# Denominators of linear attention: eight token tiles taken ahead into the accumulation of G

## The chip, the cores and the metric

The kernel runs on one core of a Trainium2 chip. A core has a matrix engine (TensorE, PE in the profile, with weight loads as PEld), three engines for vectors (VectorE or DVE, ScalarE or ACT, GpSimd or POOL), and a queue that issues transfers (SyncE, SP). Each engine works through its own list of instructions in order, and waits on semaphores where an operand comes from another engine. The metric is the time of one execution on the device in microseconds. Before the change it is 810.38 us, the median of three runs (808.94 to 812.14).

## The reference

Two kinds of layers alternate over x, of 2048 tokens by 640 features in fp32: Fourier mixing and linear attention, each twice, each behind a layer norm and with a residual.

```python
def _A_ref(x, dft_seq_re, dft_seq_im, dft_hid_re, dft_hid_im):
    a = einsum("bsd,ed->bse", x, dft_hid_re)
    b = einsum("bsd,ed->bse", x, dft_hid_im)
    return einsum("ts,bse->bte", dft_seq_re, a) - einsum("ts,bse->bte", dft_seq_im, b)

def _B_ref(x, wqkv, wo):                       # 32 heads of 20 features
    q, k, v = heads of x @ wqkv
    phi = lambda t: where(t > 0, t + 1, exp(t)) + 1e-6
    pq, pk = phi(q), phi(k)
    kv = einsum("bhsd,bhse->bhde", pk, v)
    z = einsum("bhsd->bhd", pk)                # sum of the keys over all tokens
    num = einsum("bhqd,bhde->bhqe", pq, kv)
    den = einsum("bhqd,bhd->bhq", pq, z)[..., None] + 1e-6
    return (num / den, heads joined) @ wo

x = x + A(layernorm(x)); x = x + B(layernorm(x))
x = x + A(layernorm(x)); x = x + B(layernorm(x))
```

The change concerns `den`: for each token and head, the product of the token's 20 query features with z, summed, plus 1e-6.

## The kernel before, in words

The tokens lie in 16 tiles of 128 partitions by 640 features, and stay in SBUF throughout. Matrix products that need fp32 are made of three products of a high and a low part (`split`: ACT copies the high part, DVE subtracts it to get the low one). The Fourier layers fold the tokens into symmetric parts first; folding for the second Fourier layer runs beside the outputs of the first attention layer, mostly on POOL and DVE, with statistics on ACT.

One attention layer (`Attention.keys_values`) works in these stages:

- Keys and queries for a group of tiles. The first group has ten tiles (0 to 9), the second six (10 to 15). A tile is normed, transposed, multiplied by the key weights and by the query weights, and both go through phi. Query tiles are kept (`self.PQ`); the query of the last tile is left for later (`late`). POOL adds each key tile to a running sum, `pksum` (line 295).
- G for the same group (`gram`, line 251): 30 matmuls a tile take the normed tile transposed with its keys into four PSUM buffers. DVE norms the tile once more (line 127), ACT and DVE make high and low parts of the tile (xh, xl) and of its keys (ph, pl; lines 133 and 134); this is `gram_ready`, called one tile ahead. xn, xh, xl and ph take four of the 12 buffers of the temporary pool (`temp`, tag "tmp").
- With tile 10, the first of the second group, `total` adds ten small matmuls (line 350) that sum `pksum` over the partitions into unused columns of the same PSUM buffers. After the second group `total_out` copies these sums with ACT into a tile zb (lines 359 and 360): z, the same in every partition.
- Combining (`combine`): G is combined with the value weights (line 390) and masked by heads, and then multiplied by the output weights, of which ACT and DVE make the parts. The result is the matrix M of a layer. In between stand the late query and the first weighted queries.
- Outputs (`outputs`): tile by tile, the weighted query is transposed, split, multiplied by M, and DVE adds the result to x (line 490).

A weighted query takes two functions. `weigh` (line 434) multiplies the query by zb on POOL. `weighted` reduces the product over the 20 features of a head to 32 denominators per token (line 447, DVE), adds 1e-6 (line 448, DVE), takes reciprocals (line 449) and multiplies the query by them in two pieces (lines 451 and 457). `weigh` is called three tiles ahead of the output it is for, `weighted` two tiles ahead.

The order in which the instructions of an engine stand is not the order of the source: the tile framework schedules them by a simulated timeline and priorities, which `k.ahead(...)` shifts for single steps (the table `AHEAD`). Only SP's order is by hand, and in the Fourier parts the vector engines'. Buffers of a pool are handed out in turn, and a new tile in a buffer waits for the last use of the old one.

In layer 0, DVE also compares symmetric halves of the Fourier matrices piece by piece (`Check`, lines 1033 and 1050), in steps placed among the tiles; `verdict` evaluates this in the last stage.

Of the kernel before, what the change touches and what calls it, by code (L numbers as in the profile page):

```python
# [8 lines left out]
F32 = mybir.dt.float32  # L9
F32R = mybir.dt.float32r  # L10
AF = mybir.ActivationFunctionType
ALU = mybir.AluOpType
AX = mybir.AxisListType

S, D, H, DH = 2048, 640, 32, 20
# [29 lines left out]
VLOWS = (0, 0, 1, 0)  # L45
WLOWS = ((5, 2), (1, 1))
GATE = 2
AHEAD = {'0out00': -60, '2keep00': -60, '2out10': -600, '1q13': 60, '2keep01': 600, '2keep02': 5, '0kv0': 5, '2out02': -20, '0out10': -600, '0keep00': -5, '1q14': 60, '0w1': 5, '2out01': 20, '0kv2': -600, '0m1': -5, '0kv5': 60, '1weigh15': -20, '0out12': -200, '1res13': 5, '2m1': -20, '0keep10': 60, '0weigh0': 60, '0first': -5, '2out12': -200, '2weigh1': 5, '2first': 60, '0m3': 20, '2out13': -200}


class K:
    def __init__(self, tc, ctx):
        self.tc, self.nc = tc, tc.nc
        nc = self.nc
        self.n = self.layer = self.part = 0
        self.cst = ctx.enter_context(tc.tile_pool(name="cst", bufs=1))
        self.psp = ctx.enter_context(tc.tile_pool(name="ps", bufs=4, space=bass.MemoryType.PSUM))
        self.ident = self.cst.tile([128, 128], F32, name="ident")
        make_identity(nc, self.ident)
        self.ones = self.cst.tile([128, 128], F32, name="ones")  # L60
        nc.vector.memset(self.ones, 1.0)
        self.mhalf = self.cst.tile([128, 1], F32, name="mhalf")
        nc.vector.memset(self.mhalf, -0.5)

# [4 lines left out]
    def after(self, later, earlier):  # L69
        self.tc.add_manual_dep(  # L70
            later.ins,
            earlier.ins.name,
            mybir.DependencyInfo(mybir.DependencyClass.Sync, mybir.DependencyReason.DATA),
        )

    def ahead(self, what, *at):

        n = AHEAD.get(f"{self.part}{what}" + "".join(str(i) for i in at), 0)
        return self.tc.high_priority(offset=n) if n else nullcontext()
# [70 lines left out]
def halves(pu):  # L150
    return pu.rearrange("p (a b) -> p a b", a=2)[:, :, :HD]


def h2(t):
    return t.rearrange("p (a b) -> p a b", a=2)
# [16 lines left out]
class Attention:  # L172
    def __init__(self, k, X, order, order2, wqkv, wo, mask, saved=None):
        self.k, self.X, self.order, self.order2, self.mask, self.saved = k, X, order, order2, mask, saved
        self.wqkv, self.wo, self.W = wqkv, wo, {}
        self.kept = {}

    def wt(self):
        return self.k.wp.tile([128, 640], F32R, tag="w", name=self.k.nm("w"))
# [83 lines left out]
    def keys_values(self, check=None, keep=1, saves=()):  # L263

        saves = list(saves)
        k, nc, W = self.k, self.k.nc, self.W
        pksum = k.temp()
        nc.gpsimd.memset(pksum, 0.0)
        self.PQ, late = {}, []
        if check is not None:  # L270
            check.fetch()

        def proj(part, x):
            pu = k.psum()
            product(nc, pu, *x, [w[0] for w in W[part]], [w[1] for w in W[part]])
            return pu

        def phi(pu, out):
            e = k.temp()
            nc.scalar.activation(h2(e), halves(pu), AF.Relu, scale=-1.0)  # L280
            nc.scalar.activation(h2(out), halves(pu), AF.Relu)
            nc.scalar.activation(e, e, AF.Exp, scale=-1.0)  # L282
            nc.vector.scalar_tensor_tensor(out, e, 1e-6, out, op0=ALU.add, op1=ALU.add)  # L283

        x, acc, tail = self.x0, [], None
        for a, b in ((0, CUT), (CUT, NT)):
            pks = []
            for n in range(a, b):
                with k.ahead("normed", n + 1):
                    xn = self.normed(n + 1) if n + 1 < NT else None  # L290
                pk = self.slot()
                pu = proj(1, x)
                with k.ahead("key", n):
                    phi(pu, pk)
                nc.gpsimd.tensor_tensor(pksum, pksum, pk, op=ALU.add)  # L295
                pks.append(pk)
                if xn is not None:
                    tp = k.transposed(xn)
                    with k.ahead("chunks", n):
                        x2 = k.split_chunks(tp)  # L300

                def query(i=self.order[n], x=x):
                    pq = k.pqp.tile([128, D], F32, tag="pq", name=k.nm("pq"))
                    pu = proj(0, x)
                    with k.ahead("query", i):
                        phi(pu, pq)
                    self.PQ[i] = pq

                if n < NT - keep:
                    query()  # L310
                else:
                    late.append(query)
                if n > 0 and saves:
                    self.save(*saves.pop(0))
                if check is not None and n in STEPS[0]:
                    check.step(True)
                if n == b - 2:
                    with k.ahead("gram", a):
                        ready = self.gram_ready(a, pks[0])
                if xn is not None:  # L320
                    x = x2
            G = [k.psum() for _ in range(3)]
            tail = tail or k.psum()
            for n in range(a, b):
                with k.ahead("gram", n + 1):
                    nxt = self.gram_ready(n + 1, pks[n + 1 - a]) if n + 1 < b else None
                self.gram(G + [tail], ready, n == a, n == b - 1, a == 0)
                if n == CUT:
                    self.total(G, pksum)
                if check is not None and n in STEPS[1]:  # L330
                    check.step(n != STEPS[1][-1])
                ready = nxt
            if a == 0:
                acc = [self.slot() for _ in range(ND)]
                for c in range(ND):
                    (nc.scalar.copy if c % 2 else nc.vector.tensor_copy)(acc[c][:, :GA], self.place(G, c, 0))
                nc.scalar.copy(acc[ND - 1][:, GA:], self.place(G, ND - 1, 1))
        self.total_out(G)
        for c in range(ND):
            nc.vector.tensor_tensor(acc[c][:, :GA], acc[c][:, :GA], self.place(G, c, 0), op=ALU.add)  # L340
        c = ND - 1
        nc.vector.tensor_tensor(acc[c][:, GA:], acc[c][:, GA:], self.place(G, c, 1), op=ALU.add)
        for c in range(ND - 1):
            nc.scalar.copy(acc[c][:, GA:], self.place([None] * 3 + [tail], c, 1))
        self.combine(acc, late)
# [16 lines left out]
    def combine(self, G, late):  # L362
# [65 lines left out]
            self.M.append(m)  # L428
        self.next, self.t1 = qd, self.weigh(2)

    def weigh(self, n):
        k = self.k
        t1 = k.temp()
        k.nc.gpsimd.tensor_tensor(t1, self.PQ[self.order2[n]], self.zb, op=ALU.mult)  # L434
        return t1

    def weighted(self, n, t1):

        k, nc, pq = self.k, self.k.nc, self.PQ[self.order2[n]]
        heads = lambda t: t.rearrange("p (h d) -> p h d", d=DH)
        den, rden = (
            k.sm.tile([128, H], F32, tag="sm" + n, name=k.nm(n), bufs=2) for n in ("den", "rden")
        )
        nc.vector.tensor_reduce(den, heads(t1), axis=AX.X, op=ALU.add)
        nc.vector.tensor_scalar(den, den, 1e-6, None, op0=ALU.add)
        nc.vector.reciprocal(rden, den)
        chunks = t1.rearrange("p (i c) -> p i c", i=ND)  # L450
        nc.vector.tensor_tensor(
            chunks[:, :, :EC].rearrange("p i (h d) -> p i h d", d=DH),
            pq[:, : EC * ND].rearrange("p (i h d) -> p i h d", i=ND, d=DH),
            rden[:, : 6 * ND].rearrange("p (i h) -> p i h", i=ND).unsqueeze(3).to_broadcast([128, ND, 6, DH]),
            op=ALU.mult,
        )
        nc.vector.tensor_tensor(
            chunks[:, :, EC:].rearrange("p i (h s) -> p h i s", h=2),
            pq[:, EC * ND :].rearrange("p (h i s) -> p h i s", h=2, i=ND),
            rden[:, 6 * ND :].unsqueeze(2).unsqueeze(3).to_broadcast([128, 2, ND, 4]),  # L460
            op=ALU.mult,
        )
        return t1

    def outputs(self, after, between=lambda: None):
# [4 lines left out]
        for n, i in enumerate(self.order2):  # L470
# [16 lines left out]
            for pu, hs in zip(pus, parts):  # L487
# [3 lines left out]
                after(i, hs[0], hs[-1] + 1)  # L491
            if n == NT - GATE:
                late = last
# [850 lines left out]
```

## Time and profile before

| | |
|---|---|
| median of three runs | 810.38 us (808.94 to 812.14) |
| the profiled execution | 809.75 us |
| its span | 808.0 us |
| mean granted TensorE clock | 0.993 |
| PE busy | 745.8 us, 92% |
| DVE busy | 615.9 us, 76% |
| ACT busy | 338.2 us, 42% |
| POOL busy | 318.6 us, 39% |

The span runs from the first instruction to the last. In it layer 0's attention takes from about 130 to 428 us, layer 1's from about 490 to the end. Times of rows are in microseconds from the span's start, the mean of a group in nanoseconds. A row of a timeline names start, length, engine, line, operation, output and input tiles, and in brackets how long the engine was idle before it and what ended that. A row of the chain of waits names start, length, engine, tile and line. A row of the waits names who waited, for whom, and the total, the number and the longest. A row of groups ends with busy time, mean of one, and idle time before.

### The profile page before, as it was taken

The numbers are of one execution on the slowest core, as the hardware profiler recorded it, in microseconds if no ns is written. First come the engines' busy times: TensorE is split into PE (matmuls) and PEld (weight loads), VectorE is DVE, ScalarE is ACT, GpSimd is POOL, SyncE is SP. The second block draws the span as 40 slices with busy tenths as digits, with TensorE's granted clock in tenths as the row PEclk, the third lists the DMA queues.
The fourth block names the chain that finished last, engine by engine and source line by source line (L and its number), as shares of the span: only waits on it lengthen the run. The fifth ranks groups of instructions, "written<-read, shape, count | busy, mean of one in ns | idle before, by whom it ended". The sixth has DMA issues, their size and how long they took to land.

```text
span 808.0 us, 12986 instructions
## 1 busy us (share of the span) xinstructions
PE 745.8 (92%) x4920; PEld 708.3 (88%) x4920; DVE 615.9 (76%) x1153; ACT 338.2 (42%) x592; POOL 318.6 (39%) x354
## 2 busy tenths in 40 slices
PE   0579999999999999999898998999999999999997
PEld 0238899999999999899784888999999999989997
DVE  7799988865963575989978789776597386499982
ACT  4534544446324554455552424544633445341110
POOL 5987991211021111369894755211101111134310
PEclk9989999999999999999999999999999999999999
DMA  9122327880450422000004552544044024001121
GB/s 330 53 85 66 116 77 222 237 272 34 140 173 1 141 82 82 20 1 1 1 1 147 197 197 88 164 154 141 1 140 141 1 71 143 21 12 50 66 83 70
DMA packets 36008, 81.25 MB, mean 101 GB/s; under 512 B 4142, under 2 KB 5937, under 8 KB 35936
## 3 DMA queue, kind: packets, MB, share of 16 engines
q1 hardware_dynamic: 35904, 80.27, 31.4%
q8 instruction: 41, 0.67, 0.4%
q14 instruction: 31, 0.25, 0.1%
q0 software_dynamic: 32, 0.06, 0.0%
HBM read 68.10 MB, written 11.80 MB: 99 GB/s over the span
## 4 chain that ended last, share of the span: by engine, by line
PE 65%; DVE 17%; POOL 10%; issue 3%; ACT 2%; DMA 2%; SPq 0%; DVEq 0%; POOLq 0%; ACTq 0%
PE ps L167 41%; PE ps L251 16%; PE ps L139 3%; PE ps L935 2%; PE ps L390 2%; DVE w L134 1%; DVE x L960 1%; POOL t L434 1%; POOL w L134 1%; DVE t L134 1%; POOL ab L738 1%; POOL ab L743 1%; POOL ab L613 1%; DMA rawc<-in_so 1%; DMA x<-in_x 1%
## 5 line engine op out<-in xcount | busy, mean ns | idle before, releaser
L167 PE MATMUL ps<-w,t 128*128 128x320 f32 x2880 | 440.6, 311 | 8.1 <-DVE t L134 5.9
L167 PEld LDWEIGHTS ps<-w,t 128*128 128x128 f32 x2880 | 423.0, 188 | 11.3 <-DVE t L134 8.3
L295 POOL TENSOR_TENSOR t<-t,s 128x640 f32<-128x640 f32 x32 | 58.5, 1829 | 224.1 <-DVE s L283 216.1
L251 PE MATMUL ps<-t,t 128*128 128x256 f32 (+1 forms) x640 | 140.1, 310 | 0.0
L280 ACT ACTIVATE t<-ps 128x640 f32<-128x640 f32 x64 | 45.2, 706 | 160.3 <-PE ps L167 160.3
L251 PEld LDWEIGHTS ps<-t,t 128*128 128x128 f32 x640 | 107.4, 188 | 0.0
L1050 DVE CUSTOM_DVE_ANT_0 junk<-ck,ck 128x688 bf16<-128x688 f32 (+4 forms) x138 | 99.8, 723 | 9.4 <-DMA ck<-in_ck 7.6
L251 PE MATMUL ps<-w,t 128*128 128x384 f32 (+1 forms) x320 | 98.7, 310 | 0.0
L434 POOL TENSOR_TENSOR t<-pq,t 128x640 f32<-128x640 f32 x32 | 56.0, 1757 | 101.8 <-ACT t L360 48.7
L134 DVE TENSOR_TENSOR t<-ps,t 128x640 fp32r<-128x640 f32 (+1 forms) x66 | 53.8, 816 | 40.8 <-ACT t L133 40.5
L133 ACT CAST t<-ps 128x640 fp32r<-128x640 f32 (+1 forms) x66 | 45.6, 692 | 66.3 <-PE ps L139 57.9
L892 PE MATMUL ps<-cw,ab 128*107 128x512 f32 (+4 forms) x108 | 42.7, 532 | 32.4 <-DVE ab L633 26.0
L892 PEld LDWEIGHTS ps<-cw,ab 128*107 128x107 f32 (+1 forms) x108 | 18.3, 181 | 51.4 <-issue 48.0
L283 DVE SCALAR_TENSOR_TENSOR pq<-t,pq 128x640 f32<-128x640 f32 x32 | 30.6, 956 | 40.4 <-ACT t L282 40.4
L251 PEld LDWEIGHTS ps<-w,t 128*128 128x128 f32 x320 | 60.2, 188 | 0.1
L139 PE MATMUL ps<-ident,t 128*128 128x128 f32 x320 | 45.7, 273 | 6.8 <-DVE t L127 2.6
L935 PE MATMUL ps<-t,u 107*128 107x322 f32 (+1 forms) x306 | 49.6, 321 | 1.6 <-DVE u L917 1.6
L935 PEld LDWEIGHTS ps<-t,u 107*128 107x128 f32 (+1 forms) x306 | 47.3, 195 | 3.2 <-DVE u L917 2.7
L282 ACT ACTIVATE t<-t 128x640 f32<-128x640 f32 x64 | 48.1, 751 | 0.0
L139 PEld LDWEIGHTS ps<-ident,t 128*128 128x128 f32 x320 | 38.0, 140 | 9.3 <-DVE t L123 2.6
L127 DVE TENSOR_SCALAR t<-x,kept 128x640 f32<-128x640 f32 x58 | 43.1, 744 | 1.0 <-PE ps L251 0.9
L134 DVE TENSOR_TENSOR t<-t,t 128x640 fp32r<-128x640 f32 x32 | 26.3, 822 | 21.8 <-ACT t L133 21.4
(178 smaller groups left out, 998.0 us busy)
## 6 DMA issues: line engine op xcount, KB each, us to landing
ck<-in_ck SPq DMA_DIRECT2D x48, 346.0 KB
ck<-in_ck SPq DMA_DIRECT2D x48, 344.0 KB
save<-w SPq DMA_DIRECT2D x20, 320.0 KB
w<-save SPq DMA_DIRECT2D x20, 320.0 KB
x<-in_x SPq DMA_DIRECT2D x16, 320.0 KB
out<-x SPq DMA_DIRECT2D x15, 320.0 KB
raw<-in_wqkv SPq DMA_DIRECT2D x10, 320.0 KB
s<-in_wqkv SPq DMA_DIRECT2D x10, 320.0 KB
```

The lines of the kernel that those rows point to most:

```text
L133: self.nc.scalar.copy(hi, src)
L134: self.engine(pool).tensor_tensor(lo, src, hi.bitcast(F32), op=ALU.subtract)
L139: self.nc.tensor.transpose(tp[:, 128 * c : 128 * c + 128], src[:, 128 * c : 128 * c + 128], self.ident)
L167: nc.tensor.matmul(pu[:m, 512 * h : 512 * h + HD], s, w[:, HD * h : HD * h + HD], start=first, stop=last)
L251: nc.tensor.matmul(self.place(G, c, part), x[:, 128 * c : 128 * c + 128], p[:, f : f + n], start=start and i == 0, stop=stop and i == 2, s ...
L280: nc.scalar.activation(h2(e), halves(pu), AF.Relu, scale=-1.0)
L282: nc.scalar.activation(e, e, AF.Exp, scale=-1.0)
L295: nc.gpsimd.tensor_tensor(pksum, pksum, pk, op=ALU.add)
L434: k.nc.gpsimd.tensor_tensor(t1, self.PQ[self.order2[n]], self.zb, op=ALU.mult)
L892: nc.tensor.matmul(pu[:m, o : o + n], e, w[:, f : f + n], start=g == 0 and i == 0, stop=g == end and not more and i == len(both) - 1,)
L935: self.k.nc.tensor.matmul(po[:, o : o + 322], s[:m, f : f + 128], w[:m, x, :], start=first, stop=last)
L1050: i = nc.vector.tensor_tensor_reduce(k.junk[:, : a.shape[1]], b, a, 1.0, 0.0, op0, op1, o)
```

## The change

`total_out` is called right after `total`, with tile 10 of the second group, instead of after the group. Behind it a new function `denominators` takes the first nine tiles in the order of the outputs and, for those whose query is already there (eight: the late query is tile 6 of that order), multiplies by zb on POOL as before, adds the upper ten features of each head to the lower ten on POOL, reduces the remaining ten on DVE, and adds 1e-6 on POOL. The eight times 32 values go to a tile of their own. For these tiles `weigh` later only hands out a buffer, and `weighted` begins with the reciprocal. For the other eight tiles the product and the reduction are as before, but ACT adds the 1e-6, from a constant tile `eps` that a memset on DVE fills at the start.

```diff
+EARLY = 9
...
+        self.eps = self.cst.tile([128, 1], F32, name="eps")
+        nc.vector.memset(self.eps, 1e-6)
...
                 if n == CUT:
                     self.total(G, pksum)
+                    self.total_out(G)
+                    self.denominators()
...
-        self.total_out(G)
         for c in range(ND):
             nc.vector.tensor_tensor(acc[c][:, :GA], acc[c][:, :GA], self.place(G, c, 0), op=ALU.add)
...
+    def denominators(self):
+
+        k, nc = self.k, self.k.nc
+        all_den = k.sm.tile([128, H * EARLY], F32, tag="early", name=k.nm("early"), bufs=1)
+        for n in range(EARLY):
+            if self.order2[n] in self.PQ:
+                self.early(n, all_den[:, H * n : H * n + H])
+
+    def early(self, n, den):
+        k, nc = self.k, self.k.nc
+        t1 = self.weigh(n)
+        self.den[n] = den
+        t = t1.rearrange("p (h d) -> p h d", d=DH)
+        nc.gpsimd.tensor_tensor(t[:, :, :10], t[:, :, :10], t[:, :, 10:], op=ALU.add)
+        nc.vector.tensor_reduce(den, t[:, :, :10], axis=AX.X, op=ALU.add)
+        nc.gpsimd.tensor_scalar(den, den, 1e-6, None, op0=ALU.add)
+
     def weigh(self, n):
         k = self.k
         t1 = k.temp()
+        if n in self.den:
+            return t1
         k.nc.gpsimd.tensor_tensor(t1, self.PQ[self.order2[n]], self.zb, op=ALU.mult)
         return t1
...
-        nc.vector.tensor_reduce(den, heads(t1), axis=AX.X, op=ALU.add)
-        nc.vector.tensor_scalar(den, den, 1e-6, None, op0=ALU.add)
+        if n in self.den:
+            den = self.den[n]
+        else:
+            nc.vector.tensor_reduce(den, heads(t1), axis=AX.X, op=ALU.add)
+            nc.scalar.activation(den, den, AF.Identity, bias=k.eps)
         nc.vector.reciprocal(rden, den)
```

More of the change, by code (lines that the diff above doesn't have):

```diff
@@ L175, in __init__ @@
         self.wqkv, self.wo, self.W = wqkv, wo, {}
-        self.kept = {}
+        self.kept, self.den = {}, {}
     def wt(self):
```

## The prediction

> **What bounds the kernel now.** I read the busy time by stage first, then the chain of waits over the second token group, then the timelines of POOL, VectorE (DVE) and ScalarE (ACT) there. Stages of layer 0 (three rows) and layer 1 (three): second group in G, combining, outputs. A row holds the stretch, its length, busy time and (count) of PE, its weight loads, DVE, ACT and POOL, then granted clock, DMA share and GB/s.
>
> ```profile
> 291.00:319.00 28.00, 27.52 (x190) 27.31 (x189) 17.29 (x30) 11.89 (x23) 2.00 (x1) 1.00 0.35 112
> 319.00:344.00 25.00, 23.28 (x174) 21.40 (x173) 24.78 (x51) 10.39 (x21) 11.50 (x6) 1.00 0.09 21
> 344.00:428.00 84.00, 76.17 (x516) 72.95 (x515) 74.44 (x115) 44.87 (x89) 70.79 (x97) 1.00 0.04 10
> 675.00:704.00 29.00, 28.50 (x196) 28.29 (x195) 15.36 (x22) 13.09 (x24) 2.01 (x1) 1.00 0.37 114
> 704.00:730.00 26.00, 24.25 (x178) 21.77 (x177) 25.97 (x50) 10.34 (x21) 12.73 (x7) 1.00 0.05 10
> 730.00:808.00 78.00, 72.34 (x510) 71.99 (x509) 59.25 (x96) 9.03 (x13) 15.29 (x10) 0.99 0.18 69
> ```
>
> TensorE (PE) bounds every one. What it loses is small: 0.5 us in each G stage, 1.72 and 1.75 in combining, 7.83 in layer 0's outputs; the 5.66 of the last row lie after its last matmul (below: 802.36). DVE is as full as PE in combining and, like POOL, nearly so in layer 0's outputs. In the G stages POOL is empty (2.00 of 28), which is where the change puts its work.
>
> ```profile
> 195.18 44.14 PE ps L251 x300
> 295.48 1.38 PE ps L350 x10
> 296.86 21.89 PE ps L251 x149
> 318.75 4.37 PE ps L167 x30
> 681.67 22.01 PE ps L251 x149
> 793.54 8.82 PE ps L167 x60
> ```
>
> Ten tiles take 44.14 us, so one takes 4.41: 15 products of 384 columns and 15 of 256, some 0.176 and 0.118 each. The second group runs without a gap, 296.86 to 318.75.
>
> **What the change adds in G, step by step.** Building the changed program gives the order in which its instructions stand, and for each wait the instruction waited for. POOL's queue, once zb is there: six products w0 to w5, half-add h0, w6, w7, h1 to h5, e0 (the 1e-6), h6, h7, e1 to e7. The waits that matter (tile 12 is the third of the group):
>
> ```
> ACT  xh of tile 12 (hi of x)    waits for reduce 0 (DVE), which waits for h0
> DVE  xl of tile 12              waits for reduce 1, which waits for h1; both stand before it in the queue
> ACT  ph of tile 12 (hi of key)  waits for xl of tile 12
> PE   tile 12, 1st product       waits for ph;  its 5th product waits for pl
> DVE  queue: xl12, reduce 2, reduce 3, xn13, pl12, (check), reduce 4, 5, reciprocal (waits for e0),
>      reduce 6, (check), xl13, reduce 7, reciprocal (waits for e1), xn14, pl13
> ```
>
> The first two waits come from the temporaries: 12 buffers, eight now held by the early products, so tile 12's xh and xl take over buffers of products 0 and 1 after their reductions. Before, nothing of this stood between tile 11 and tile 12. Prices, from POOL, DVE and ACT in the timelines:
>
> ```profile
> 293.42 2.00 POOL L295 TENSOR_TENSOR t<-t,s 128x640 f32<-128x640 f32 x1 [6.82 <-DVE s L283]
> 319.69 4.06 POOL L434 TENSOR_TENSOR t<-pq,t 128x640 f32<-128x640 f32 x2 [24.27 <-ACT t L360]
> 340.39 1.56 POOL L434 TENSOR_TENSOR t<-pq,t 128x640 f32<-128x640 f32 x1 [4.82 <-DMA w<-t]
> 351.19 0.88 POOL L738 TENSOR_TENSOR ab<-t 128x319 f32<-128x319 f32 x1 [1.19 <-ACT t L125]
> 352.01 0.19 POOL L739 COPY ab<-t 128x2 f32<-128x2 f32 x1
> ...
> 293.93 1.84 DVE L127 TENSOR_SCALAR t<-x,kept 128x640 f32<-128x640 f32 x1
> 296.62 0.82 DVE L134 TENSOR_TENSOR t<-t,t 128x640 fp32r<-128x640 f32 x1
> 297.36 0.61 DVE L127 TENSOR_SCALAR t<-x,kept 128x640 f32<-128x640 f32 x1
> 298.62 0.33 DVE L1033 TENSOR_REDUCE ca<-ck 128x1 f32<-128x173 f32 x1
> 298.87 0.87 DVE L1050 CUSTOM_DVE_ANT_0 junk<-ck,ck 128x692 bf16<-128x692 f32 x1
> 321.07 1.27 DVE L134 TENSOR_TENSOR w<-raw,w 120x640 fp32r<-120x640 f32 x1
> 336.21 0.80 DVE L447 TENSOR_REDUCE den<-t 128x32 f32<-128x640 f32 x1
> ...
> 303.28 0.72 ACT L133 CAST t<-s 128x640 fp32r<-128x640 f32 x1
> 318.41 0.41 ACT L359 COPY t<-ps 128x256 f32<-128x256 f32 x1
> 319.30 0.32 ACT L360 COPY t<-ps 128x128 f32<-128x128 f32 x1
> ```
>
> A product alone takes 1.56 us (2.03 in pairs beside busy DVE; DVE mostly waits here, so I take 1.56). No row shows POOL adding 32 runs of ten; the nearest has half a row flat, 0.88, and the full row's 1.56 is the other end. I take 0.86, since these cost by elements, and keep 1.56 for the range. A reduction of 320 elements: half of 0.80, so 0.45 with its start. A DVE subtraction is 0.82 alone, 1.27 beside POOL, so 1.1 during the half-adds; the normalization 0.61 alone, 1.84 beside POOL, so 1.2. e is like the smallest POOL rows, 0.2.
>
> Layer 0 on the old clock. Tile 10 ends at 294.9; 12 products of tile 11 now go ahead of the total (1.4 us), to 296.3, so PE no longer waits 0.48 for POOL's last key sum, done at 295.42. The total takes 1.38, to 297.7. Its three copies by ACT (0.41, 0.41, 0.32) overlap it and end at 298.3. Writes of tile 11 now wait for these copies; each ends before it is needed, so I cost that at nothing; without the overlap it would be 1.1 us. Tile 11 is through at 300.7.
>
> POOL: six products from 298.3, to 307.7; h0 to 308.5; w6 and w7 to 311.6; h1 to 312.5. DVE: reduce 1 to 313.0, xl to 314.1. ACT: ph to 314.9. PE therefore stands from 300.7 to 314.9. It does four products, then waits for pl: two reductions to 315.0 (h3 is done at 314.2), xn13 to 316.2, pl12 to 317.3. The other 26 products are 3.77 us at full clock.
>
> **The clock after such a stall.** Late in the first Fourier stage PE was idle for three microseconds:
>
> ```profile
> 48.00:50.00 2.00, 0.93 (x3) 1.00 0.23 62
> 50.00:52.00 2.00, 0.00 (x0) 1.00 0.32 93
> 52.00:54.00 2.00, 1.98 (x6) 0.63 0.19 46
> 54.00:56.00 2.00, 1.06 (x3) 0.50 0.45 108
> 58.00:60.00 2.00, 2.00 (x7) 0.66 0.82 261
> 60.00:62.00 2.00, 1.61 (x10) 1.00 0.32 75
> ```
>
> The granted clock then fell to 0.50 and was back at 1.00 some 6.5 us after work resumed. After a gap of 14 us I expect the same: half speed until 314.9 + 6.5 = 321.4. From 317.3 to there PE does 2.0 us of work, and the last 1.75 end at 323.1, 2.0 later than at full clock. [...]
>
> Layer 1 has the same order without the check. After pl12 DVE needs reduce 4 and 5 (0.9), a reciprocal (0.3), xl13 (0.8), reduce 6 (0.45), pl13 (0.8): 320.5, in time for 323.1. Tiles 13 to 15 follow at 4.41 each, to 336.4. Against 318.75 that is **+17.6 us** (layer 1's own group takes 22.01 against 21.89, so its clock carries over).
>
> In layer 0 DVE also has 0.33 + 0.87 of the check ahead of reduce 4 and 0.87 ahead of xl13, reduce 7, a reciprocal and xn14 (0.6) ahead of pl13: 317.3 + 1.1 + 0.9 + 0.3 + 0.45 + 0.87 + 0.8 + 0.45 + 0.3 + 0.6 + 0.8 = 323.9. PE waits for that with 26 products left: tile 13 ends at 327.7, tiles 14 and 15 at 336.6, **+17.8 us**. Nothing covers these two terms: they delay PE, and everything behind is PE's own work.
>
> **What the change takes away.** The rows of waits and groups for the stages behind:
>
> ```profile
> PE ps L167 <- DVE t L134: 5.0, 4, 2.1
> PE ps L892 <- DMA cw<-in_co: 1.6, 1, 1.6
> PE ps L167 <- ACT t L133: 1.0, 2, 0.7
> ...
> 290.00:344.00 54.00, 11.50 (x6) 1.00 0.24 69
> 344.00:428.00 84.00, 16.48 (x10) 1.00 0.04 10
> ...
> 344.00:428.00 84.00, 8.90 (x11) 1.00 0.04 10
> ...
> L448 DVE TENSOR_SCALAR den<-den 128x32 f32<-128x32 f32 x32 | 18.9, 594 | 0.4
> ```
>
> Of layer 0's 16 products six already ran before 344 and ten (second row) in the outputs, of its 16 reductions eleven (the last row of windows). The changed order keeps eight of each in the outputs: two products (3.1 us) less for POOL, three reductions (2.4) and all additions of 1e-6 (0.59 each, 18.9 / 32) less for DVE. Against it, each of the eight late tiles has DVE wait for ACT between reduction and reciprocal: some 0.32 + 0.14 by the smallest ACT row. PE's waits there that other engines end are 6.0 us; I expect 2.5 back (nothing and 6.0 are the ends). In combining POOL is free and DVE loses about four reductions of 25 us; 0.8 back per layer (ends 0 and 1.7). In the last stage PE has nothing to give back, and DVE's slack (59 of 78) hides the hand-over. The memset of eps is one small instruction at the start, behind loads. No DMA is added or moved; SP's order is the same.
>
> **Sum.** 17.8 + 17.6 − 2.5 − 1.6 = +31.3. The profiled execution took 809.75 us (span 808.0), the median of the runs 810.38; 809.75 + 31.3 gives **841 us**.
>
> **Rivals.**
> 1. *Half-adds at the price of a full row.* Runs of ten might cost POOL 1.56. Four of them lie ahead of pl12, eight ahead of pl13: +2.8 in layer 1, +5 in layer 0; with products at the contended 2.03 (eight, +3.8 a layer) 856. For it: no row of this shape. Against it: DVE waits rather than competes. [...]
> 2. *Short stall.* The clock stays full, pl12 comes sooner, layer 0's outputs give back all 6.0 and combining 3.4: 841 − 2 − 2.5 − 3.5 − 1.8 = 831.
> 3. *Faster.* PE never waits in G because the half-adds reach their place in time; then only the gains count, 809.75 − 1.0 − 4.1 = 805, at best 800. It decides if h1 ends by 298.7, two microseconds ahead of 300.7; with zb ready at 298.3, nine POOL operations before h1 and its own, 14 us, stand against it. It would need the buffers of tile 12 to be others than the program's waits say.
>
> **How the numbers follow.** My forecast, a stall of about 14 us in both layers, has 0.84; rival 1 beyond 853 has 0.06, rival 2 below 830 has 0.05, rival 3 has 0.04 and about no change 0.01. Range 829 to 853: below, rival 2 (831) and a little; above, most of the way to rival 1's 856. A change of 0.5% (4 us) is about what a measurement of this kernel can tell from none. Faster 0.04, same 0.01, slower 0.95.
>
> **What would show it.** After the total, POOL without a gap for about 22 us; PE idle some 14 us between tile 11 and tile 12, ended by ACT's ph, and again 1 to 2 us for DVE's pl, in both layers; the granted clock at half just after; layer 0's tile 13 waiting for DVE, layer 1's not; the second group at about 40 us instead of 22; outputs of layer 0 shorter by 2 to 3 us. Wrong would be: tile 12 starting near 301 (then the waits were misread), POOL half-adds far from 0.86, or the outputs changing by more than 6 us.

## The result and the profile after

The changed kernel takes 847.14 us, the median of four runs (840.77 to 848.67), beside 810.76 for the kernel before (808.94 to 812.14): a ratio of 1.0391, with a 95% interval of 1.0336 to 1.0447. It is slower, as forecast, and inside the range; the number given was 841. The profiled execution took 848.67 us (span 846.9, granted clock 0.969).

One thing must be known about the times: executions of one and the same program, the kernel before among them, lie in two groups some 6 us apart (of 62 of the kernel before that ran beside the experiments, 31 took 808.7 to 812.1 and 31 took 813.8 to 819.1). The likely reason is a wait at about 104 us, called the early wait below, that the last section shows: it stands in three of the thirteen profiles (the changed kernel and runs 3 and 4). No execution of the kernel before from its upper group was profiled, so that the wait makes these groups too is inferred. The four runs of the kernel before in the result lie with the lower group (up to 812.14), so the ratio contains the early wait of the changed kernel. So stages are compared here, and totals only where that wait is named.

The views of busy time for the same five stretches, before and then after. Each begins with the same matmul: first of the second group in G of layer 0, late query, first of the next Fourier stage, first of the second group of layer 1, late query. The columns are those of the prediction's first fence.

```profile
290.30:318.59 28.29, 27.81 (x192) 27.60 (x191) 17.46 (x31) 11.99 (x22) 2.00 (x1) 1.00 0.37 113
318.59:426.77 108.18, 98.64 (x688) 94.18 (x687) 98.39 (x163) 55.67 (x111) 82.29 (x103) 1.00 0.04 11
426.77:675.09 248.32, 242.23 (x1586) 230.86 (x1587) 179.86 (x370) 105.90 (x177) 74.61 (x88) 1.00 0.37 115
675.09:703.52 28.43, 27.93 (x193) 27.72 (x191) 14.79 (x21) 12.61 (x23) 2.01 (x1) 1.00 0.38 116
703.52:808.00 104.48, 97.08 (x690) 94.25 (x688) 85.70 (x146) 19.85 (x35) 28.02 (x16) 0.99 0.15 54
```

```profile
297.63:344.68 47.05, 31.69 (x192) 30.77 (x191) 23.11 (x44) 12.18 (x22) 27.07 (x25) 0.82 0.20 62
344.68:447.99 103.31, 97.65 (x688) 94.17 (x687) 82.23 (x133) 57.78 (x119) 68.67 (x95) 1.00 0.05 14
447.99:697.76 249.77, 243.72 (x1587) 232.29 (x1587) 180.01 (x371) 105.84 (x177) 75.19 (x88) 0.99 0.37 115
697.76:744.41 46.65, 31.25 (x192) 30.33 (x191) 20.68 (x34) 12.58 (x23) 26.04 (x25) 0.82 0.20 62
744.41:846.90 102.49, 96.09 (x690) 94.23 (x688) 65.75 (x118) 23.01 (x43) 12.66 (x8) 1.00 0.16 59
```

Both groups in G grow, by 18.76 and 18.22 us; POOL's 24 to 25 us of new work stand in them, and PE's busy time grows by 3.9 and 3.3 at a granted clock of 0.82. What is given back is small: 4.87 us in combining and outputs of layer 0, 1.99 in layer 1, though DVE is relieved of 16 and 20 us there. The third stretch is 1.45 longer (the experiments spread over 247.1 to 249.5 in it). The first stretch already begins 7.33 later than before: the early wait. Together 18.76 + 18.22 − 4.87 − 1.99 + 1.45 + 7.33 = 38.9, which is the difference of the spans.

Inside the group of layer 0, PE's timeline of the changed kernel (only instructions that PE waited for; in brackets how long, and for whom), and the first of the same in layer 1:

```profile
303.50 0.39 PE L254 MATMUL ps<-w,t 128*128 128x256 f32 x1 [1.16 <-DVE w L137]
322.68 1.54 PE L254 MATMUL ps<-t,t 128*128 128x256 f32 x4 [13.46 <-ACT t L136]
324.95 0.58 PE L254 MATMUL ps<-w,t 128*128 128x256 f32 x1 [0.73 <-DVE w L137]
...
722.82 1.54 PE L254 MATMUL ps<-t,t 128*128 128x256 f32 x4 [13.49 <-ACT t L136]
```

The timelines of POOL, ACT and DVE over that wait:

```profile
306.61 9.28 POOL L457 TENSOR_TENSOR t<-pq,t 128x640 f32<-128x640 f32 x6 [3.84 <-ACT t L364]
315.85 0.78 POOL L448 TENSOR_TENSOR t<-t 128x320 f32<-128x320 f32 x1
316.59 3.02 POOL L457 TENSOR_TENSOR t<-pq,t 128x640 f32<-128x640 f32 x2
319.59 4.62 POOL L448 TENSOR_TENSOR t<-t 128x320 f32<-128x320 f32 x5
...
317.24 0.73 ACT L136 CAST t<-t 128x640 fp32r<-128x640 f32 x1 [10.71 <-DVE early L449]
321.90 0.72 ACT L136 CAST t<-s 128x640 fp32r<-128x640 f32 x1 [3.93 <-DVE t L137]
...
316.66 0.49 DVE L449 TENSOR_REDUCE early<-t 128x32 f32<-128x320 f32 x1 [6.63 <-POOL t L448]
320.39 0.49 DVE L449 TENSOR_REDUCE early<-t 128x32 f32<-128x320 f32 x1 [3.24 <-POOL t L448]
320.98 0.83 DVE L137 TENSOR_TENSOR t<-t,t 128x640 fp32r<-128x640 f32 x1
323.48 1.42 DVE L137 TENSOR_TENSOR w<-s,t 128x640 fp32r<-128x640 f32 x1
```

This is the chain of the prediction, link by link: six products, h0, two products, h1 on POOL; reduce 0 lets ACT make xh (317.24); reduce 1 lets DVE make xl (320.98); xl lets ACT make ph (321.90); ph lets PE go (322.68). What follows is the clock (busy time of stretches: PE standing, PE standing at half clock, PE working at half clock; at 330.84 the clock is full again):

```profile
309.22:313.78 4.56, 0.00 (x0) 0.00 (x0) 0.78 (x1) 0.00 (x0) 4.56 (x4) 1.00 0.00 0
313.78:322.68 8.90, 0.00 (x1) 0.01 (x1) 2.39 (x5) 1.45 (x2) 8.90 (x9) 0.50 0.00 0
322.68:330.84 8.16, 7.43 (x26) 6.92 (x27) 8.16 (x18) 2.18 (x3) 7.59 (x10) 0.50 0.13 38
```

By an estimate from the halved clock, 7.43 us of work would have been 3.7 at full clock, so 3.7 are lost. The 18.76 are then 13.46 + 0.73 (waits) + 3.7 (clock) + 0.68 (a first wait of 1.16 for the low part of tile 11's key, in place of 0.48 for the key sum) = 18.6.

### The profile page after: what moved, and what is told of

Its sections match the earlier page's. It is cut to its first block, busy times and chain, and to the rows that moved or that the text cites. A ratio compares the mean times of both kernels' runs of the same rounds, so it can differ in the third digit from the quotient of the medians.

```text
span 846.9 us, 12997 instructions
## 1 busy us (share of the span) xinstructions
PE 750.7 (89%) x4920; PEld 715.0 (84%) x4920; DVE 593.4 (70%) x1122; ACT 343.4 (41%) x608; POOL 336.7 (40%) x386
## 4 chain that ended last, share of the span: by engine, by line
PE 64%; DVE 13%; POOL 13%; issue 4%; ACT 3%; DMA 2%; SPq 0%; POOLq 0%; DVEq 0%; ACTq 0%
PE ps L170 43%; PE ps L254 15%; POOL t L457 4%; PE ps L142 3%; PE ps L961 2%; DVE x L986 2%; PE ps L394 1%; POOL ab L764 1%; DVE t L130 1%; POOL ab L769 1%; POOL t L448 1%; POOL ab L639 1%; POOL mv L117 1%; DMA x<-in_x 1%; DVE t L477 1%
## 5 line engine op out<-in xcount | busy, mean ns | idle before, releaser
L170 PEld LDWEIGHTS ps<-w,t 128*128 128x128 f32 x2880 | 426.1, 189 | 6.4 <-DVE t L137 5.5
L254 PE MATMUL ps<-t,t 128*128 128x256 f32 (+1 forms) x640 | 145.7, 318 | 26.9 <-ACT t L136 26.9
L254 PEld LDWEIGHTS ps<-t,t 128*128 128x128 f32 x640 | 111.4, 195 | 27.4 <-ACT t L136 27.4
L254 PE MATMUL ps<-w,t 128*128 128x384 f32 (+1 forms) x320 | 101.5, 319 | 3.8 <-DVE w L137 3.8
L457 POOL TENSOR_TENSOR t<-pq,t 128x640 f32<-128x640 f32 x32 | 50.4, 1589 | 77.2 <-PE ps L170 65.8
L254 PEld LDWEIGHTS ps<-w,t 128*128 128x128 f32 x320 | 62.5, 195 | 5.4 <-DVE w L137 5.2
L286 DVE SCALAR_TENSOR_TENSOR pq<-t,pq 128x640 f32<-128x640 f32 x32 | 27.1, 847 | 51.2 <-ACT t L285 51.2
L130 DVE TENSOR_SCALAR t<-x,kept 128x640 f32<-128x640 f32 x58 | 45.9, 791 | 12.5 <-PE ps L254 12.5
L516 DVE TENSOR_TENSOR x<-x,ps 128x640 f32<-128x640 f32 (+1 forms) x34 | 26.3, 773 | 22.2 <-PE ps L170 22.1
```

The lines of the kernel that those rows point to most:

```text
L130: self.nc.vector.tensor_scalar(out, x, m, rs, op0=ALU.subtract, op1=ALU.mult)
L170: nc.tensor.matmul(pu[:m, 512 * h : 512 * h + HD], s, w[:, HD * h : HD * h + HD], start=first, stop=last)
L254: nc.tensor.matmul(self.place(G, c, part), x[:, 128 * c : 128 * c + 128], p[:, f : f + n], start=start and i == 0, stop=stop and i == 2, s ...
```

## The experiments

My theory: tile 12's parts take over buffers of early products, and so wait for POOL's half-adds. Rivals: POOL's work beside the group slows DVE; the early copies of the total, or the hand-over of the 1e-6 to ACT, cost; the early wait belongs to the change. Each run was profiled once. The stages of all profiles, in us, begin with the same matmuls as above (from PE's timelines; the last column ends with the span). "Median" is of all runs of that kernel.

| kernel | median (runs) | group start | group, layer 0 | combining, outputs | next stages | group, layer 1 | combining, outputs |
|---|---|---|---|---|---|---|---|
| before | 810.76 (4) | 290.30 | 28.29 | 108.18 | 248.32 | 28.43 | 104.48 |
| changed | 847.14 (4) | 297.63 | 47.05 | 103.31 | 249.77 | 46.65 | 102.49 |
| 1: 1e-6 on ACT only | 813.55 (10) | 290.14 | 28.29 | 105.91 | 247.62 | 28.28 | 104.86 |
| 2: and total's copies early | 807.47 (10) | 291.07 | 29.00 | 104.70 | 247.90 | 28.98 | 104.05 |
| 3: change, two own slots | 819.30 (10) | 296.30 | 33.01 | 105.21 | 248.72 | 32.99 | 102.57 |
| 4: change, no half-adds | 832.18 (4) | 295.86 | 41.86 | 103.11 | 249.28 | 37.62 | 102.37 |
| 5: change, four tiles | 829.34 (2) | 290.97 | 38.02 | 105.60 | 249.09 | 37.59 | 103.13 |
| 6: as 3, with fills | 820.33 (8) | 292.90 | 33.03 | 104.95 | 249.48 | 31.50 | 103.94 |
| 7: as 1, three splits moved | 806.01 (10) | 289.93 | 28.29 | 105.87 | 247.13 | 28.34 | 103.54 |
| 8: as 1, two splits moved | 804.60 (4) | 287.56 | 28.32 | 105.58 | 248.24 | 28.31 | 103.49 |
| 9: change, two splits moved | 836.29 (4) | 288.03 | 46.92 | 103.19 | 248.58 | 45.73 | 102.45 |
| 10: denominators after the group | 813.54 (10) | 288.49 | 29.07 | 107.27 | 248.70 | 29.02 | 108.45 |
| 11: 8 once more | 805.62 (7) | 289.15 | 28.31 | 105.69 | 248.99 | 28.31 | 103.65 |

**1. The 1e-6 alone.**

```diff
-                    self.total_out(G)
-                    self.denominators()
...
+        self.total_out(G)            # back behind the group
         for c in range(ND):
```

> Only the hand-over of the 1e-6 to ACT is kept; the copies of the total and all denominators stand where they stood before. My theory (the loss is the early denominators' buffers) expects no stall in either G group (late query at most 1 us later than before on the same clock) and 807 to 811.5 us. A rival that puts part of the loss on DVE waiting for ACT in each tile of the outputs expects layer 0's outputs (before: first transposition 342.84 to the next Fourier stage at 426.77) to grow by 2 us or more, and 813 us or more. For the seven us that the changed kernel lost at about 104 us, ahead of everything the change touches: if the new constant tile or the program's new layout causes it, it is here too; if it is chance, it is here only with luck.

The groups are those of the kernel before, and layer 0's combining and outputs are 2.27 us shorter, not longer. The group row of the new instruction:

```profile
L473 ACT ACTIVATE den<-den,eps 128x32 f32<-128x32 f32 x32 | 10.2, 318 | 38.4 <-DVE den L472 34.7 <-DVE ckflag L1109 3.7
```

ACT pays 0.32 us each where DVE paid 0.59. So about half of what the change gives back in layer 0 (4.87) comes with the hand-over, without any early denominator; runs 7, 8 and 11, which have the same hand-over, show the same stretch at 105.6 to 105.9. In layer 1 nothing is gained (104.86 against 104.48). Of its ten runs three took 805.8 to 808.5 and seven 812.8 to 815.7: two groups as in the kernel before. Their median, 813.55, lies above the expected 807 to 811.5 and on the rival's side, but the stages decide against the rival. The ratio over all (0.9985, 0.9941 to 1.0029) mixes both groups.

**2. The total's copies early, no denominators.** (`self.denominators()` is left out of the change.)

> The total's copies stand early, inside the second group, and the 1e-6 is ACT's, but no denominator is computed early. My theory expects PE to wait about 1.2 us for the lower half of tile 11's key in place of 0.5 for the key sum, no other wait in the group, so +0.7 a layer, and 808 to 813 us. A rival by which the early copies (PE's writes behind ACT's reads) hold PE expects 3 us or more per layer between tile 11 and tile 12, and 816 or more.

Each group is 0.6 to 0.7 us longer, by PE's 1.16 for tile 11, and has no other wait: the copies hold nobody. The median, 807.47, lies just below the expected 808 to 813; the ratio, 0.9932 (0.989 to 0.9974), mixes both groups of times. Layer 0's combining and outputs are 3.48 us shorter than before here, layer 1's 0.43, again without an early denominator. Of the 4.87 and 1.99 that the change gives back, 1.4 and 1.6 are left for the early denominators themselves, less than the 4.0 us a group that run 3 below still loses by them.

**3. The products in slots of their own.**

```diff
+        pair = [self.slot() for _ in range(2)]
...
-        t1 = self.weigh(n)
+        nc.gpsimd.tensor_tensor(t1, self.PQ[self.order2[n]], self.zb, op=ALU.mult)   # t1 is pair[n % 2]
```

> All eight early denominators are kept, with the same products, half-adds, reductions and additions, but the products go through two weight slots of their own in turn, so that no temporary of tile 12 has to wait for a reduction. My theory expects the 13.5 us stall gone in both layers, at most 2 us of waits in each G group, outputs and combining as short as in the changed kernel, and 801 to 812 us. The rival, that POOL's 22 us of work beside the group slows DVE's splits through what the two share, expects the stall to stay in good part (8 us or more a layer) and 825 or more, since POOL's work is the same.

The 13.5 us are gone: the groups take 33.0 us, so 14 of the 18 us went with the buffers. The two slots also change POOL's pace, since a third product has to wait for a reduction: 18.93 and 21.71 us of POOL's work lie in the groups, against 27.07 and 26.04 in the change. The expected 801 to 812 were missed, though, since 4 us a group stay beside run 2 (median 819.3, the early wait in the profile included). The timelines of PE and DVE show where they begin, and beneath them stand the same three DVE instructions of run 2, where POOL is idle:

```profile
310.69 0.39 PE L254 MATMUL ps<-w,t 128*128 128x256 f32 x1 [2.17 <-DVE w L137]
...
305.86 1.67 DVE L137 TENSOR_TENSOR t<-t,t 128x640 fp32r<-128x640 f32 x1 [3.23 <-ACT t L136]
307.46 1.84 DVE L130 TENSOR_SCALAR t<-x,kept 128x640 f32<-128x640 f32 x1
309.23 1.41 DVE L137 TENSOR_TENSOR w<-s,t 128x640 fp32r<-128x640 f32 x1
```

```profile
300.63 0.83 DVE L137 TENSOR_TENSOR t<-t,t 128x640 fp32r<-128x640 f32 x1 [3.23 <-ACT t L136]
301.38 0.61 DVE L130 TENSOR_SCALAR t<-x,kept 128x640 f32<-128x640 f32 x1
301.90 0.82 DVE L137 TENSOR_TENSOR w<-s,t 128x640 fp32r<-128x640 f32 x1
```

2.3 us of DVE's work become 4.9 beside POOL's first products and half-adds, each instruction 0.6 to 1.2 us longer. PE waits 2.17 us for it in layer 0, and 1.31 for tile 14's pl; in layer 1 it waits 2.15, and then works at half clock for 3.4 us. So DVE is slower beside POOL's work, as the rival said, and that is about a fifth of the loss (4 us of 18 to 19 a group). Why these three instructions are longer there (1.67, 1.84 and 1.41 us against 0.83, 0.61 and 0.82), no trace here shows.

**4. No half-adds.** DVE reduces the whole early products, and the half-adds are left out.

```diff
-        nc.gpsimd.tensor_tensor(t[:, :, :10], t[:, :, :10], t[:, :, 10:], op=ALU.add)
-        nc.vector.tensor_reduce(den, t[:, :, :10], axis=AX.X, op=ALU.add)
+        nc.vector.tensor_reduce(den, t, axis=AX.X, op=ALU.add)
```

> The half-adds are left out; DVE reduces all 640 elements of each early product (0.8 us in place of 0.45). The same buffers are taken, but tile 12 now waits only for products 0 and 1 and their reductions, some 10 us sooner in POOL's queue. My theory expects PE to stand 3 to 6 us before tile 12 in place of 13.5, the wait ended by ACT's ph of tile 12, and 811 to 822 us. If the size of the stall were set by the total of POOL's work or by the eight products alone, it would stay at 9 us or more a layer, and the time at 828 or more.

```profile
311.21 1.54 PE L254 MATMUL ps<-t,t 128*128 128x256 f32 x4 [3.76 <-ACT t L136]
...
323.57 0.39 PE L254 MATMUL ps<-w,t 128*128 128x256 f32 x1 [2.53 <-DVE w L137]
```

The wait before tile 12 shrinks to 3.76 us, as it should when only two products and two reductions stand before it. The total missed (832 instead of 811 to 822; by its group start the early wait is 5.6 of it): each group still grows by 9 to 14 us. Behind the 3.76 us come half clock (310.8 to 317.6), a wait of 1.49 for tile 12's pl, whose subtraction takes 2.16 us beside eight products in one row (15.18 us on POOL), and in layer 0 a wait of 2.53 inside tile 13. DVE's own reductions are longer here too, 0.81 us each.

**5. Four tiles instead of eight.** (`EARLY = 4`.)

> Four early denominators instead of eight, in the same temporaries as in the change. Four products and eight other temporaries just fit, so tile 12 finds free buffers and only tile 13's x and low parts wait, for reductions 0 to 2, behind four products and three half-adds on POOL instead of nine operations and more. My theory expects no wait before tile 12, a wait of 2 to 5 us inside tile 13, G groups of 31 to 35.5 us (before 28.3, changed kernel 46.9), and 811 to 821 us, or 7 us more where the early wait at about 104 us strikes. If the stall came in proportion to POOL's work, half of 18.5 us would stay in each group, at tile 12: 37.5 us, and 828 or more.

This expectation failed, and the rival's number (37.5) came out: 38.0 and 37.6. PE and DVE at tile 12:

```profile
307.60 0.58 PE L254 MATMUL ps<-w,t 128*128 128x256 f32 x1 [3.32 <-DVE w L137]
...
302.54 1.17 DVE L137 TENSOR_TENSOR t<-t,t 128x640 fp32r<-128x640 f32 x1 [5.24 <-PE ps L254]
303.63 1.83 DVE L130 TENSOR_SCALAR t<-x,kept 128x640 f32<-128x640 f32 x1
305.39 2.16 DVE L137 TENSOR_TENSOR w<-s,t 128x640 fp32r<-128x640 f32 x1
```

No half-add is waited for at tile 12, but its parts now wait for PE to let go of a buffer of an earlier tile (ACT 2.09 us, DVE 5.24), and then pl12 comes 3.32 us late behind three DVE instructions that take 5.2 us beside POOL's products and first half-add, where run 2 has 2.3. The clock halves again, from 306.5 to 313.3. I had taken "a free buffer" for "a buffer free in time", and left out DVE's length beside POOL. So the 37.5 came out without proportion as its cause: no part of tile 12 waits for a reduction.

**6. Fills between POOL's instructions.** Run 3, with a fill of one column after each product and half-add.

> The kernel with the two own slots, and after nearly each of POOL's early products and half-adds a fill of one column with zeros, which reads nothing. Without the fills DVE's subtractions and normalizations beside POOL took 1.4 to 2.2 us instead of 0.6 to 0.8, and the G groups 33.0 us. If DVE is kept waiting until POOL does something that does not read two tensors, the fills let it in: subtractions at most 1.4 us in the group, PE's waits for DVE's pl below 1.2 us each beyond the first, groups of 29 to 31.5 us. If DVE's length beside POOL has another cause, such as shared bandwidth, nothing changes: 33 us, or more by the fills' own time.

Nothing changes in layer 0 (33.03; xl12, xn13 and pl12 take 1.67, 1.88 and 1.40), and PE waits 2.19 us for tile 12's pl in both layers, where run 3 has 2.17 and 2.15. Layer 1's group is 1.5 us shorter, inside the range for the fills, but that is the clock: behind this wait it fell to half for 3.4 us in layer 1 of run 3 and not in layer 1 of run 6 (last section). In layer 0 it is the other way round: run 6 has 3.4 us at half clock, run 3 none, but the further wait of 1.31 us. So the lengths of the groups say little of the fills. The first two products stand side by side with the fills behind them, so for xl12 and xn13 the run says little; pl12, beside half-adds with a fill between them, takes 1.40 where run 3 has 1.41. So with this fill pl12 was not shorter. Why DVE's instructions are longer beside POOL's is left open.

**7 and 8. Fewer splits on POOL ahead of the early wait.** Run 1 with `WLOWS = ((2, 2), (1, 1))`, then with `((3, 2), (1, 1))`: three and two of five weight splits go to DVE.

> The hand-over of the 1e-6 to ACT alone, and in layer 0 three of the five splits of the query weights that POOL does move to DVE, which shortens POOL's unbroken row of additions and splits at 97 to 110 us. If the seven us at about 104 us come from DVE being kept waiting by that row (normalization 5.84 us instead of 1.06), no run has them any more: all runs between 803 and 809 us. If they come from something else, runs of 812 to 816 us appear about as often as before.

> As the run before, with only two of the five splits moved to DVE. By the same reasoning the row before the normalization is shorter by two splits (3.1 us): fewer runs with the early wait than the kernel with all five on POOL, and a wait of at most 4 us where it strikes; most runs 803 to 809 us.

Run 7: nine of ten runs at 805.0 to 808.4, one at 811.75, which misses the expected "all". Run 8: four of four at 802.2 to 806.6. Run 1 had only three of ten below 809, so POOL's unbroken row there has to do with the early wait; as the splits also move into DVE's queue, the row is not shown to be the cause by itself. The ratios are 0.9925 (0.9887 to 0.9962) and 0.9891 (0.9813 to 0.9968).

**9. The change with the early wait taken away.** The changed kernel with `WLOWS = ((3, 2), (1, 1))`.

> The whole change as it is, with two of layer 0's splits of the query weights moved from POOL to DVE, so that the early wait at about 104 us (7.3 us in the profile of the changed kernel) is shorter or gone. If that wait is no part of the change's own cost, this kernel takes 833 to 842 us, with the stalls of 13.5 us before tile 12 in both groups as they were and groups of 46 to 47.5 us. If the change itself costs the full 38.9 us that the two profiles differ by, it stays at 845 or more.

834.9 to 838.2, with waits of 13.45 and 13.47 us before tile 12. Layer 0's group is as it was; layer 1's is 0.9 shorter and just under the expected 46, as the clock was full again there some 5.2 us after PE's restart (711.78 to about 717.0, by the spacing of the products) instead of 7.4 (722.82 to 730.21). So the change costs its time without the early wait too. Its own cost is 38.9 − 7.3 = 31.6 us by the changed kernel's profile. By this run's it is 834.9 − 808.0 = 26.9, and 2.3 by which its first group begins sooner than in the kernel before: 29.2. Whether the change makes the early wait more frequent is open; its four runs are too few to tell.

**10. The denominators after the group.** Run 3 with two splits moved, and the first early product held until DVE has split the last key:

```diff
+        if n == 0:
+            k.after(op, self.low)     # low: DVE's split of the last tile's key
...
                     self.total_out(G)
+                if n == NT - 1:
                     self.denominators()
```

> The eight denominators in two slots of their own, but POOL's first product waits until DVE has split the last tile's key, so that POOL's work lies beside the end of the group and the combining; the two weight splits as in the run before. If POOL's work beside DVE's splits is what is left of the loss (33.0 us for a group with own slots, 29.0 without early denominators), the groups come back to 28.5 to 29.6 us, and PE's wait of 2.2 us for tile 12's pl is gone; 799 to 806 us. If DVE, which is full in combining, pays there instead, the stretch from the late query to the next Fourier stage exceeds 107 us (105.2 with own slots) and the time is above 807.

The groups are back at 29.0, with 8 to 9 us of POOL's new work still at their ends, behind DVE's last split. So POOL's work beside DVE's splits was what was left of the loss. But the stretches behind grow to 107.27 and 108.45, and the time misses the expected 799 to 806, as the rival said: the views of busy time there, of run 8 and of this run, for layer 1:

```profile
698.01:801.50 103.49, 97.01 (x690) 94.27 (x688) 80.26 (x130) 24.72 (x51) 26.57 (x16) 0.99 0.15 55
```

```profile
702.55:811.00 108.45, 98.82 (x690) 95.56 (x688) 74.49 (x125) 23.07 (x43) 29.19 (x24) 0.98 0.15 56
```

DVE has 5.8 us less to do and the stretch is 5.0 longer. PE's longest wait for DVE's weight splits in its first part is 3.1 us, in run 8 0.2, and the clock is at half for 3.4 us just behind it: what counts there is when DVE's splits come, not how much it does. In layer 0 the stretch is 1.7 longer than run 8's. Ratio 1.0003 (0.9972 to 1.0034).

**11. Run 8 once more.**

> The fastest kernel so far once more: the 1e-6 on ACT, no early denominators, two splits moved. Expected 802 to 807 us in every run, and a ratio to the kernel before of 0.985 to 0.993.

805.0 to 808.3, a little above what was expected at the upper end; ratio 0.9909 (0.9872 to 0.9947). The 1e-6 on ACT, no early denominators, and two splits moved to DVE take about 1% less than the kernel before, over both its groups of times; the slowest of the eleven runs (8 and 11), 808.3, is still under the fastest of the 62, 808.7.

## Why the prediction was right

- *Order and waits* (six products, h0, two products, h1; xh behind reduce 0, xl behind reduce 1, ph behind xl): shown in the timelines. That the buffers caused most of it is shown by these waits and by run 3, where they are gone.
- *zb ready at 298.3*: POOL starts at 306.61, on the old clock 299.28. A wait that the prediction did not have came first: PE saves 0.48 for the key sum, as forecast, but the products that moved ahead of the total need tile 11's pl, 1.16 us late because DVE's split took 2.18 beside POOL's key sum. Run 2 has this by itself, +0.6 to 0.7 a group.
- *The copies cost nothing*: right; run 2 shows no wait by them.
- *Prices*: product 1.55 (1.56 taken), half-add 0.78 alone and 0.92 in a row (0.86), reduction 0.49 (0.45), xl and pl 0.83 and 1.42 (1.1), xn 0.66 (1.2). e took 0.78, not 0.2, and cost nothing, as it stands late in the queue. Rival 1 falls with the half-add; of rival 2 nothing came.
- *The stall*: 14.2 expected, 13.46 measured; the second wait 1.7 expected, 0.73 measured.
- *The clock* is the term that was mis-sized: 2.0 us taken, 3.7 measured. I let it return 6.5 us after the restart; it took 8.2, of which 7.4 were work. Two things were off. The stretch from which I took the 6.5 gives 7.3 when it is read in finer steps (work again from 52.02, full clock from 59.34). And I counted only the work behind the second wait; that wait was shorter than thought, so more work fell into the half clock. The errors cancel almost to nothing (14.2 + 1.7 + 2.0 against 13.46 + 0.73 + 3.7), which is luck. A fixed time from the restart, as I took it, does not hold: after nearly the same wait the clock was full 8.16 us from the restart in layer 0 (a wait of 13.46), 7.39 in layer 1 (13.49), and some 5.2 in layer 1 of run 9 (13.47).
- *Layer 0's tile 13 waiting for pl13*: did not happen. At half clock PE reaches tile 13 later than DVE is ready. Layer 0's group costs 18.76 (17.8), layer 1's 18.22 (17.6).
- *What is given back*: 4.87 in layer 0 (3.3 expected, outputs and combining together), 1.99 in layer 1 (0.8). The prediction lists what DVE and POOL lose by the early denominators and by the 1e-6 together; by run 1, 2.27 of layer 0's come with the 1e-6 alone, by run 2, 3.48 with the 1e-6 and the early copies.
- *The sum*: 31.3 expected; 29.2 (run 9) to 31.6 measured without the early wait, which is 839 to 841 us; one of the changed kernel's four runs took 840.77. The profiled 848.67 has 7.3 us more by a wait ahead of everything the change touches, which no step foresaw; the one profile of the kernel before does not have it. That 847.14 still lies in the range owes nothing to the reasoning.

What the prediction did not see stands beside the stall. I held DVE beside POOL to be a price of 0.3 to 0.6 on single instructions. It is a limit of its own: with the buffers out of the way 4 us a group remain (run 3 against run 2), so the early denominators would not pay in this place even with buffers to spare.

## What to carry to other kernels

Work that is moved to an engine that stands idle can take time of other engines too (here PE stood for 13.5 us a group): ask which buffers its results hold, who takes over those buffers next, and whether the last use comes in time; a queue that is full of one kind of work (all products, then all half-adds) makes the first release late (here the first half-add came behind six products, 9.28 us). Ask also which engine's instructions grow longer beside it, when that neighbour has just enough time (here three DVE instructions took 4.9 us in place of 2.3). And before a gain is put down to the large part of a change, time the small part alone: here ACT's 0.32 us in place of DVE's 0.59 was the useful half.

## What the runs showed of the hardware

**One DVE normalization of 5.84 us in place of 1.06.** The early wait in the changed kernel's timelines, PE, then DVE, then POOL meanwhile, and the same normalization in the kernel before:

```profile
110.80 1.30 PE L142 MATMUL ps<-ident,t 128*128 128x128 f32 x5 [7.15 <-DVE t L130]
...
100.31 3.78 DVE L986 TENSOR_TENSOR x<-x,t 128x321 f32<-128x321 f32 x1
104.82 5.84 DVE L130 TENSOR_SCALAR t<-x,kept 128x640 f32<-128x640 f32 x1
...
104.96 0.85 POOL L993 TENSOR_TENSOR x<-x,t 128x321 f32<-128x321 f32 x1
105.77 1.52 POOL L137 TENSOR_TENSOR w<-raw,w 128x640 fp32r<-128x640 f32 x1
...
109.68 0.63 POOL L271 MEMSET t<- 128x640 f32 x1
```

```profile
101.97 1.06 DVE L127 TENSOR_SCALAR t<-x,kept 128x640 f32<-128x640 f32 x1
```

The normalization takes 5.84 us, over four of POOL's additions (three of 0.85 us each are left out here), a split and a fill, and ends 0.35 us after the fill; an addition on DVE takes 3.78 instead of 0.74. POOL's instructions are not longer meanwhile (the split 1.52 us; in the kernel before 1.55 to 1.83 in this place). The same 5.84 us stand in the profiles of runs 3 and 4; in the other ten profiles this normalization takes 1.05 to 1.90. Beside the early work of run 3 DVE's normalizations took at most 1.85 and its subtractions at most 2.17. Why it is so much longer in this place was not settled. That it comes and goes from one execution of the same program to the next is what the two groups of times suggest.

**Waits of some 2.2 us, with and without half clock behind them.** PE stood for 2.15 us in layer 1 of run 3 and for 2.19 us in layer 1 of run 6, both for pl12. Busy time of stretches: run 3 standing, and working soon after; run 6 working after its wait; and run 4 working after its 2.53 us in layer 0, from 0.85 us after the restart:

```profile
695.46:697.61 2.15, 0.00 (x0) 0.00 (x1) 2.15 (x3) 1.29 (x2) 2.15 (x3) 1.00 0.30 76
698.44:701.86 3.42, 3.42 (x15) 3.42 (x14) 3.42 (x7) 0.73 (x1) 1.15 (x2) 0.50 0.02 5
694.76:699.00 4.24, 4.24 (x29) 4.24 (x30) 4.24 (x7) 1.03 (x3) 1.87 (x5) 1.00 0.02 4
324.42:327.83 3.41, 3.41 (x15) 3.41 (x14) 3.41 (x10) 0.73 (x1) 0.77 (x1) 0.50 0.00 0
```

In run 3 the clock is full while PE stands, and at half for 3.42 us from 698.44 on, 0.83 us after the restart. In run 6 it stays full over the 4.24 us behind the wait; behind the same wait of 2.19 us in layer 0 of run 6 it was at half for 3.4 us. So waits of nearly one length were followed by half clock or by none, and the half clock could begin after work had resumed; what decides it was not settled here. Half clock lasted 3.41 us in the changed kernel at 511.75 (to 515.17), 6.82 in the Fourier stage of the kernel before (52.52 to 59.34) and some 6.8 at tile 12 of runs 4 and 5, 10.24 from within the early wait of the changed kernel (105.57 to 115.81), and 17.07 in each of its two stalls (313.78 to 330.85, 713.14 to 730.21).
